# Filling products of TensorE: 256 columns instead of 512, a lower limit on the planned gap, and the whole run

## Chip, cores and metric

One core of a Trainium2 chip runs the program. The time is the device time of one execution in microseconds (us); "the time" of a kernel is the median of its runs. The engines are named as in the profile: PE is TensorE (matrix products), PEld its weight loads, DVE is VectorE, ACT is ScalarE, POOL is GpSimd, SP is the queue that starts the transfers (DMA). PEclk is the share of the full TensorE clock that was granted: 1.00 is 2.4 GHz, 0.50 is 1.2 GHz.

## What is computed

A recurrent attention (RWKV) over 768 steps for 4 batches of 8 heads with 48 channels, and on its output a mixture of four attention experts, two of which are taken per token.

```python
def _attn_ref(r, k, v, w, u):
    for t in range(S):                                  # S = 768
        cur = np.einsum('bhd,bhe->bhde', u[None] * kt, vt)
        y[:, :, t] = np.einsum('bhd,bhde->bhe', rt, state + cur)
        state = wt[:, :, :, None] * state + np.einsum('bhd,bhe->bhde', kt, vt)

def _moe_ref(x, w_gate, wq, wk, wv, wo):                # x: 4 x 768 x 384
    logits = x @ w_gate                                 # 4 experts, the best 2 kept
    for e in range(E):
        q, k, v = x @ wq[e], x @ wk[e], x @ wv[e]       # 64 wide
        a = softmax(causal(scale * (q @ k.T)))
        out += gate[..., e] * (a @ v @ wo[e])
```

## The kernel before

The 768 steps of a batch are cut into two units of 384. For each of the eight units the kernel first does the recurrence in chunks of 64 steps, head pair by head pair (four pairs, a function `one` for each and `far` for two of them), and then the expert stage (`moe`) of the same tokens; the recurrence of unit k+1 is interleaved with the expert stage of unit k.

A head pair of the recurrence goes: load of `lt` (decay, keys, queries; three buffers) and `nat`; two scans on DVE, `suf` (L415) and `pre` (L419); the products `kt` (L422) and `mr` (L424, written into `pre`) on DVE or POOL; on PE the transposes `ktp` (L471), the small products `aps` (L483), `ups` (L502), `yb` (L545), `yi` (L558), and in the first unit `rp` (L439), which reads `lt`; on DVE the state steps `ss` (L510), `am` (L489) and `xi` (L568); then a split into a high and a low part and a transfer `xx<-xs` (L591). The expert stage goes: projections `pp` (L643) and `vp` (L666), scores `sp` (L734), maximum and exponential (L740, L746), transposes `tp` (L759), `yp` (L790), gate (`gp`, `gb`, L824, L835) and output `op` (L862).

The order of all this is worked out on the host by `Plan.order`: each operation has a cost on each engine that may do it, and the planner lays the operations out in time, engine by engine. Every engine then runs its instructions in that order, and semaphores hold an instruction until its inputs and its buffer are there. The planner notes two things of each operation: `o["gap"]`, a pair of the time at which its engine becomes free and the time at which the operation is planned to begin, and `o["new"]`, the buffers that the operation is the first to use, each with the time at which it comes free. PSUM has eight banks, all under one tag (`mo`). On PE an operation whose kind of product differs from the one before is planned 100 ns later (`DRAIN`).

When the instructions are emitted (L928 to L942), a PE operation that opens a PSUM bank can be preceded by filling products: products of a constant (`wz`, zeros and ones in bf16) into the bank that the operation is about to overwrite. They compute nothing that is used. Their number follows from the planned gap t, counted from the later of "PE free" and "bank free". In the kernel before, this is done only where the gap is over 1000 ns and PE becomes free before 60 us of planned time; each product has 512 columns, is counted as 216 ns, and 600 ns at the end of the gap are left empty. At the beginning, 14 products of the same kind (`warm`, L908) run before any real work.

Of the kernel before, what the change touches and what calls it, by code (L numbers as in the profile page):

```python
# [11 lines left out]
F32 = mybir.dt.float32  # L12
# [212 lines left out]
def rwkv_moe(ctx: ExitStack, tc: tile.TileContext, wkr, nat, uN, uT,  # L225
             wqk, wvg, wo, out):
    nc = tc.nc
# [55 lines left out]
    for i in range(NYS):  # L283
        t = cst.tile([128, NH * D + C - D], F32, name=f"ys{i}")
# [620 lines left out]
    wz = one_suf.bitcast(BF16)[:, 0:512]  # L905
# [22 lines left out]
    for o in plan.order(dict(PE=7200.0 - 216 * WARM[0], DVE=1500.0, ACT=2100.0, POOL=3300.0, SP=740.0), SLACK):  # L928
        if o["e"] == "PE" and any(s.bank for _, s in o["new"]):
            at, s = next(x for x in o["new"] if x[1].bank)  # L930
            a, t = o["gap"]
            t -= max(a, at)
            if s.dt == F32 and t > 1000 and a < 60000:
                for _ in range(int((t - 600) / 216)):
                    nc.tensor.matmul(s()[:, 0:512], wz[:, 0:128], wz, start=True, stop=True)
        r = o["fn"](o["e"])
        if r is not None and o["kind"] in BOTH.get(o["e"], ()):
            if o["e"] == "DVE":
                held = r.ins
            elif held is not None:  # L940
                tc.add_manual_dep(r.ins, held.name, mybir.DependencyInfo(mybir.DependencyClass.Sync, mybir.DependencyReason.SCHED_ONLY),
                                  reason="one reader of SBUF's second port at a time")  # L942
# [109 lines left out]
```

## Time and profile before

| | |
|---|---|
| three runs | 346.18, 349.37, 351.52 us; median 349.37 us |
| the profiled execution, its own time | 345.97 us |
| its span, first to last instruction | 344.2 us |
| mean granted TensorE clock | 0.985 |
| busy: PE, DVE, ACT, POOL | 94%, 89%, 69%, 42% of the span |
| filling products (L935) | 49, all between 18.5 and 43 us |

The span lies inside the profiled execution's own time; 1.8 us lie around it. Busy times come from the profiled execution alone. The end of a product in the trace is modelled and lies behind the moment at which the next product can start, so the idle times given in brackets are shorter than the time in which PE has nothing to issue.

### The profile page before, as it was taken

What the parts mean: (1) busy time and instruction counts of PE and PEld (TensorE: products, weight loads), DVE (VectorE), ACT (ScalarE), POOL (GpSimd) and SP (SyncE); (2) the same over time, 40 slices, a digit from 0 to 9 for tenths busy, and PEclk for the clock granted to TensorE, in tenths of its full rate; (3) what the DMA queues carried; (4) which work ended last, traced back from release to release, by engine and by line L of the source; (5) the groups of instructions that cost most, each with busy time, mean ns of one, the idle gap of its engine ahead of it and who ended that gap; (6) DMA issues with size and microseconds to landing.
All of it is one profiled execution on the core that took longest, in us unless ns stands there. A gap on an engine that the chain in (4) does not pass through costs nothing.

```text
span 344.2 us, 13063 instructions
## 1 busy us (share of the span) xinstructions
PE 322.4 (94%) x5118; PEld 266.2 (77%) x5118; DVE 305.5 (89%) x1003; ACT 237.7 (69%) x726; POOL 145.7 (42%) x275
## 2 busy tenths in 40 slices
PE   7698969899999899999999999999999889999996
PEld 2555559679877788897787888898797769898884
DVE  7979979998999989999989999999999998646861
ACT  1686675976778867874966675974885567735872
POOL 3025353652852447423844444646854344121110
PEclk9769999999999999999999999999999999999999
DMA  7562855522624526161726342562543300300101
GB/s 280 176 216 60 269 150 172 164 48 71 211 104 151 182 83 214 36 196 26 233 75 196 104 141 81 154 194 79 166 146 72 116 4 4 105 0 4 70 0 70
DMA packets 15759, 41.50 MB, mean 121 GB/s; under 512 B 2385, under 2 KB 7634, under 8 KB 15698
## 3 DMA queue, kind: packets, MB, share of 16 engines
q1 hardware_dynamic: 15698, 40.67, 37.8%
q8 instruction: 40, 0.66, 0.8%
q14 instruction: 21, 0.17, 0.1%
HBM read 33.58 MB, written 4.72 MB: 111 GB/s over the span
## 4 chain that ended last, share of the span: by engine, by line
PE 68%; DVE 18%; DMA 4%; ACT 3%; issue 3%; SPq 1%; POOL 1%; DVEq 0%; POOLq 0%; ACTq 0%
PE pp L643 13%; PE yp L790 10%; PE tp L759 10%; PE vp L666 8%; PE op L862 8%; PE sp L734 7%; DMA lt<-in_wkr_dram 3%; DVE a L740 3%; PE aps L483 3%; DVE ss L510 2%; PE yi L558 2%; PE yb L545 2%; PE ups L502 2%; DVE suf L415 2%; DVE pre L419 2%
## 5 line engine op out<-in xcount | busy, mean ns | idle before, releaser
L746 ACT ACTIVATE a<-a,mx 128x128 f32<-128x128 f32 (+5 forms) x96 | 63.9, 668 | 12.8 <-DVE mx L740 12.4
L643 PE MATMUL pp<-xx,wh_qk 128*128 128x384 f32 (+2 forms) x216 | 57.7, 333 | 1.4 <-DMA xx<-xs 1.1
L759 PE MATMUL tp<-ident,a 128*128 128x128 f32 x336 | 48.3, 278 | 3.5 <-ACT a L746 1.1
L459 ACT ACTIVATE am<-ident,rk 128x64 f32<-128x64 f32 x174 | 44.7, 339 | 9.2 <-DVE rk L452 8.8
L759 PEld LDWEIGHTS tp<-ident,a 128*128 128x128 f32 x336 | 37.6, 141 | 10.0 <-ACT a L746 2.3
L740 DVE CUSTOM_DVE_ANT_0 a<-sp,cmask 128x384 f32<-128x384 f32 (+4 forms) x96 | 43.6, 497 | 0.4 <-PE sp L734 0.2
L643 PEld LDWEIGHTS pp<-xx,wh_qk 128*128 128x128 f32 x216 | 38.5, 188 | 2.3 <-DMA xx<-xs 1.3
L243 ACT COPY ATa<-tp 128x512 f32<-128x512 f32 (+3 forms) x73 | 32.5, 474 | 6.8 <-PE tp L759 6.8
L510 DVE SCALAR_TENSOR_TENSOR ss<-ss,suf,ups 112x48 f32<-112x48 f32 x160 | 35.9, 258 | 1.3 <-PE ups L502 0.3
L790 PE MATMUL yp<-ATa,v_sb 128*64 128x384 f32 (+2 forms) x256 | 35.0, 413 | 0.1
L643 PE MATMUL pp<-xx,wl_qk 128*128 128x384 f32 (+2 forms) x108 | 35.0, 324 | 0.0
L448 POOL TENSOR_TENSOR nat<-nat,u_sb 128x288 f32<-128x288 f32 x26 | 20.8, 804 | 33.2 <-PE yi L558 8.0
L422 POOL TENSOR_TENSOR kt<-lt,suf 128x384 f32<-128x384 f32 x24 | 23.8, 997 | 24.6 <-PE yb L545 14.4
L415 DVE TENSOR_TENSOR_SCAN suf<-lt,one_suf 128x390 f32<-128x390 f32 x32 | 31.1, 977 | 2.8 <-DMA lt<-in_wkr_dram 2.6
L419 DVE TENSOR_TENSOR_SCAN pre<-lt,inv_pre 128x390 f32<-128x390 f32 x32 | 31.0, 969 | 0.1
L666 PE MATMUL vp<-wh_vg,xx 128*128 128x260 f32 x144 | 29.6, 291 | 0.0
L790 PEld LDWEIGHTS yp<-ATa,v_sb 128*64 128x64 f32 x256 | 16.4, 136 | 14.4 <-issue 11.1
L734 PE MATMUL sp<-Kh,Qh 64*128 64x384 f32 (+4 forms) x128 | 26.5, 361 | 0.9 <-DVE ss L510 0.7
L666 PEld LDWEIGHTS vp<-wh_vg,xx 128*128 128x128 f32 x144 | 23.5, 189 | 0.1
L734 PE MATMUL sp<-Kl,Qh 64*128 64x384 f32 (+4 forms) x128 | 23.6, 325 | 0.0
L734 PE MATMUL sp<-Kh,Ql 64*128 64x384 f32 (+4 forms) x128 | 22.8, 319 | 0.0
L579 POOL TENSOR_TENSOR xx<-xi,xx 112x384 fp32r<-112x384 f32 x16 | 16.1, 1013 | 11.8 <-ACT xx L577 6.4
(354 smaller groups left out, 816.7 us busy)
## 6 DMA issues: line engine op xcount, KB each, us to landing
lt<-in_wkr_dram SPq DMA_DIRECT2D x31, 579.5 KB, 4.9
nat<-in_nat_dram SPq DMA_DIRECT2D x28, 432.0 KB, 3.7
out_dram<-ob SPq DMA_DIRECT2D x24, 192.0 KB, 1.9
xx<-xs SPq DMA_DIRECT2D x48, 48.0 KB, 2.2
w_qk<-in_wqk_dram SPq DMA_DIRECT2D x1, 768.0 KB, 6.5
nat<-in_nat_dram SPq DMA_DIRECT2D x4, 152.0 KB, 5.5
w_vg<-in_wvg_dram SPq DMA_DIRECT2D x1, 390.0 KB, 5.5
lt<-in_wkr_dram SPq DMA_DIRECT2D x1, 384.0 KB
```

Source lines behind the costliest of these rows:

```text
L243: nc.scalar.copy(o, i)
L415: plan.add("suf", {"DVE": t_scan(wb)}, lambda e: nc.vector.tensor_tensor_scan(rev(suf(), wb), rev(w_(), wb), rev(one_suf, wb), 0.0, op0=AL ...
L419: plan.add("pre", {"DVE": t_scan(wb)}, lambda e: nc.vector.tensor_tensor_scan(pre()[:, 0:wb - 1], w_()[:, 0:wb - 1], flat(inv_pre[:, 0:nh] ...
L459: nc.scalar.mul(am()[:, h, i], ident2, rk()[:, i, h:h + 1])
L510: nc.vector.scalar_tensor_tensor(sv(c + 1), zero[0:112] if c == s0 == 0 else sv(c), sfv()[0:112, c, 0:1], ups[c % 2]()[0:112, c // 2 * D:( ...
L643: nc.tensor.matmul(pp()[:, 0:W], w[:, qk, k, cs], xx()[:, x, k, x0:x0 + W], start=(k == j == 0), stop=(k == j == 2))
L666: nc.tensor.matmul(vp()[:, 0:260], xx()[:, x, k, o], w[:, k, :], start=(k == j == 0), stop=(k == j == 2))
L734: nc.tensor.matmul(sps[x]()[:, 0:w], q()[p, t], k()[p, o], start=j == 0, stop=j == 2)
L740: plan.add("max", {"DVE": t_dve(w) + T_RED}, lambda e, x=x, a=a, mx=mx, h=h, o=o, m=m, sps=sps: nc.vector.tensor_tensor_reduce(a()[:, o], ...
L746: plan.add("exp", {"ACT": t_exp(n)}, lambda e, x=x, y=y, mx=mx, a=a: nc.scalar.activation(a()[:, 0:n], a()[:, 0:n], AF.Exp, bias=mx[-1](), ...
L759: nc.tensor.transpose(tp()[:, j * 128:(j + 1) * 128], a()[:, (j0 + j) * 128:(j0 + j + 1) * 128], ident)
L790: nc.tensor.matmul(yp()[e * 64:e * 64 + 64, lo:W], v_sb[ep]()[:, j, e * 64:e * 64 + 64], at, start=(j == 0), stop=(j == nj - 1))
```

## The change

The filling products become half as wide (256 columns), the planned gap needs to be over 450 ns instead of 1000 ns, the limit at 60 us of planned time goes away, and the number of products is the gap less 250 ns, divided by 110 ns, instead of the gap less 600 ns, divided by 216 ns. The plan itself, the order of all other instructions and the engines they run on stay.

```diff
             a, t = o["gap"]
             t -= max(a, at)
-            if s.dt == F32 and t > 1000 and a < 60000:
-                for _ in range(int((t - 600) / 216)):
-                    nc.tensor.matmul(s()[:, 0:512], wz[:, 0:128], wz, start=True, stop=True)
+            if s.dt == F32 and t > 450:
+                for _ in range(int((t - 250) / 110)):
+                    nc.tensor.matmul(s()[:, 0:256], wz[:, 0:128], wz[:, 0:256], start=True, stop=True)
```

## Rows read from the trace of the kernel before

**Rows 1.** The page: busy time, share of the span and number of instructions of the engines; the granted clock in 40 equal slices; and the shares of the engines in the chain that ended last.

```profile
PE 322.4 (94%) x5118; PEld 266.2 (77%) x5118; DVE 305.5 (89%) x1003; ACT 237.7 (69%) x726; POOL 145.7 (42%) x275
...
PEclk9769999999999999999999999999999999999999
...
PE 68%; DVE 18%; DMA 4%; ACT 3%; issue 3%; SPq 1%; POOL 1%; DVEq 0%; POOLq 0%; ACTq 0%
```

**Rows 2.** Windows of 1 us, PE alone: length, PE busy (instructions begun), granted clock, share of the DMA engines, GB/s.

```profile
9.00:10.00 1.00, 0.00 (x0) 1.00 0.74 307
...
12.00:13.00 1.00, 0.71 (x42) 0.93 0.00 0
13.00:14.00 1.00, 1.00 (x43) 0.50 0.95 158
...
22.00:23.00 1.00, 1.00 (x14) 0.50 0.44 154
23.00:24.00 1.00, 1.00 (x78) 0.95 0.07 26
...
27.00:28.00 1.00, 0.09 (x5) 1.00 0.57 215
...
44.00:45.00 1.00, 0.00 (x0) 1.00 0.50 163
```

**Rows 3.** The instructions of the filling line, L935: count, then shortest, median and longest duration in ns, first and last start in us, shapes.

```profile
L935 PEld LDWEIGHTS <-one_suf x49: 95/98/152, 18.5 to 42.9; 128*128 128x128 bf16 x49
L935 PE MATMUL aps<-one_suf x26: 379/379/389, 28.8 to 37.1; 128*128 128x512 bf16 x26
L935 PE MATMUL ktp<-one_suf x14: 376/379/379, 40.3 to 43.1; 128*128 128x512 bf16 x14
L935 PE MATMUL yb<-one_suf x9: 634/634/634, 18.7 to 22.1; 128*128 128x512 bf16 x9
```

**Rows 4.** Timeline of PE, 8 to 45 us: start, length, instruction, count. The four groups of filling products, and two operations behind the first.

```profile
18.71 4.05 PE L935 MATMUL yb<-one_suf 128*128 128x512 bf16 x9
22.69 1.09 PE L545 MATMUL yb<-pre,ys 48*64 48x64 f32 x48
...
25.63 0.55 PE L471 MATMUL ktp<-ident,kt 128*128 128x128 f32 x3
...
28.79 4.06 PE L935 MATMUL aps<-one_suf 128*128 128x512 bf16 x18
...
35.57 1.90 PE L935 MATMUL aps<-one_suf 128*128 128x512 bf16 x8
...
40.34 3.18 PE L935 MATMUL ktp<-one_suf 128*128 128x512 bf16 x14 [0.34 <-DVE xi L568]
```

**Rows 5.** Timeline of all engines, 30 to 52 us: the operations that the second, third and fourth group stand before, and what these wait for.

```profile
32.20 0.52 DVE L424 TENSOR_TENSOR pre<-lt,pre 128x384 f32<-128x384 f32 x1
...
32.77 0.44 PEld L483 LDWEIGHTS aps<-pre,kt 64*64 64x64 f32 x24 [0.42 <-DVE pre L424]
...
37.02 0.54 DVE L422 TENSOR_TENSOR kt<-lt,suf 128x384 f32<-128x384 f32 x1
...
37.62 0.44 PEld L483 LDWEIGHTS aps<-pre,kt 64*64 64x64 f32 x24 [0.64 <-DVE kt L422]
...
45.09 0.31 PEld L471 LDWEIGHTS ktp<-ident,kt 128*128 128x128 f32 x3 [2.06 <-POOL kt L422]
```

**Rows 6.** Waits of PE from 60 us on: engine, tile and line that waited, what for, us in total, times, longest.

```profile
PE yi L558 <- DVE am L489: 1.2, 1, 1.2
PE tp L759 <- ACT a L746: 1.1, 3, 0.7
PE tp L759 <- DVE ss L510: 1.0, 1, 1.0
PE yb L545 <- issue: 0.8, 1, 0.8
PE tp L759 <- ACT am L459: 0.7, 1, 0.7
PE sp L734 <- DVE ss L510: 0.7, 2, 0.4
PE yi L558 <- issue: 0.6, 1, 0.6
PE op L862 <- DVE ss L510: 0.4, 1, 0.4
...
PE pp L643 <- DVE xi L568: 0.2, 1, 0.2
```

**Rows 7.** Timeline, 3 to 30 us: PE operations of the first unit that had waited (idle time in brackets).

```profile
7.85 0.52 PE L471 MATMUL ktp<-ident,kt 128*128 128x128 f32 x3 [1.00 <-DVE kt L422]
...
10.16 0.55 PE L471 MATMUL ktp<-ident,kt 128*128 128x128 f32 x3 [1.29 <-DVE kt L422]
...
16.00 1.06 PE L483 MATMUL aps<-pre,kt 64*64 64x64 f32 x22 [0.81 <-DVE am L489]
```

**Rows 8.** The chain that ended last, in order of time: start, us, what. A part of the first 60 us.

```profile
16.00 0.97 PE aps L483 x20
...
17.16 0.56 PE rp L439 x17
...
17.75 5.57 DMA lt<-in_wkr_dram
...
26.51 0.43 DVE kts L245
...
28.85 3.99 PE aps L935 x18
...
34.91 6.22 DMA lt<-in_wkr_dram
...
52.49 3.27 PE vp L666 x27
```

**Rows 9.** Groups of instructions by line: the weight loads of `vp` (busy us, mean ns of one, idle before).

```profile
L666 PEld LDWEIGHTS vp<-wh_vg,xx 128*128 128x128 f32 x144 | 23.5, 189 | 0.1
```

## Prediction

> **What bounds the kernel now.** I read the page first: its busy shares, its clock and the chain that ended last [rows 1]. PE is busy for 94% of the span and holds 68% of the chain. From 50 us to the end it has hardly a free moment, so what is put on PE there either fits into a real gap or moves the end. In the first 50 us it is otherwise: the chain goes through loads of `lt`, DVE's scans and, in one place, the filling products themselves [rows 8].
>
> The clock row says how much a filling product can still bring. It has a digit under 9 only in slices 2 and 3. In windows of 1 us [rows 2] it falls in the window from 12 to 13 us (0.93), stands at 0.50 (1.2 GHz) from 13 us to 23 us and is back in the window from 23 to 24 us (0.95). Before it fell, PE had worked in short bursts with waits of 1.00 and 1.29 us between them [rows 7], one whole window without an instruction; before it rose, PE ran the first group of nine filling products back to back [rows 4]. After that every digit is 9, and stretches that are almost empty, as from 27 to 28 us and from 44 to 45 us, did not bring it down (1.00 [rows 2]). So behind 24 us there is no clock to win back in this execution; the products put there can only be free or cost.
>
> **The change, part by part.**
>
> *How many products.* The old counts [rows 3, 4] give the planned gaps: n products mean a gap t from 600 + 216n to 600 + 216(n+1) ns. With 9, 18, 8 and 14 that is 2544 to 2760, 4488 to 4704, 2328 to 2544 and 3624 to 3840 ns. By the new rule, (t - 250)/110, they become 20 to 22, 38 to 40, 18 to 20 and 30 to 32: about 110 half-wide products for 49 wide ones.
>
> New gaps in the first 60 us: those of the first unit [rows 7] got no product before, so they were planned under 1000 ns, and each can get 1 to 6. I take four gaps with three each, 12 (none, if all are planned under 450 ns; 36, if there are six with six).
>
> New gaps behind 60 us: the profile shows real waits, not planned ones, so I take the real ones as a measure [rows 6]. They are 14 waits, 7.1 us in all. A wait in brackets is short by what a product's modelled end reaches past the next start: 379 ns [rows 3] less the 222 ns below, 0.16 us. Of those listed, the two marked "issue" lie within an operation, where no planned gap can be. The six longest of the rest (1.2, 1.0, 0.7, 0.7, 0.4, 0.4) would give 10 + 8 + 5 + 5 + 2 + 2 = 32 products. With a few that the plan has and the run has not I take 40 in ten places. Bounds: none, or 85 (7.1 us and 14 times 0.16 us, 9.3 us, all filled). In all about 160, bounds about 106 and 230.
>
> *What one costs.* At full clock 18 wide ones took 3.99 us [rows 8], 222 ns each; half of that, 111 ns, is the lower bound. The nearest row of that width is `vp` with 260 columns: 27 in 3.27 us [rows 8], 121 ns, the upper bound. I take 116 ns, between the two, which is more than the 110 ns that the rule counts. At half clock nine took 3.98 us [rows 4], 442 ns each, so 221 ns for half the width.
>
> The weight load of a filling product is 98 ns, 152 ns at half clock [rows 3], almost as long as the half-wide product. I cost it at nothing: at `vp`, loads of 189 ns [rows 9] hide behind products that follow each other at 121 ns. The Trainium skill, "TensorE: Matmul & The Clock Gate", section "What overlaps and what doesn't", says that a weight load overlaps running products only when it goes to another group of rows; it speaks against half-wide products, since there are twice as many loads. The rows here disagree: both the 222 ns and the 121 ns are for products that use all rows. By the page a product would cost 98 + 116 = 214 ns; by the rows it is 116 ns, and the sum goes by these.
>
> *The four old groups.* The second is on the chain [rows 8]. The `aps` behind it began at 32.77; its input `pre` was ready at 32.72, and the 18 products ended at about 28.79 + 3.99 = 32.78 [rows 4, 5]. They fit exactly. Now 39 of 116 ns take 4.52 us and end at 33.31: 0.54 us later (38 of 111 ns: 0.24; 40 of 121 ns: 0.85). What is late next is `yb`, `yi` and `rp` behind `aps`, then the load of `lt` at 34.91, which waits for its buffer, and the chain to 41 us. I take +0.54. The third: 19 take 2.20 us and end at 37.77, against a start of `aps` at 37.62, whose `kt` came at 37.56 [rows 5]; 0.15 us late (0 to 0.4), but the chain is then in the `lt` load, from 34.91 to 41.13 [rows 8], so nothing; without that cover, the 0.15. The fourth: 31 take 3.60 us and end at 43.94, while `ktp` waits for POOL's `kt` until 45.09 [rows 5]; nothing. The first runs at half clock: 21 of 221 ns take 4.64 us instead of 3.98, 0.66 us more. Behind it `ktp` ended at 26.18 [rows 4], and DVE's copy `kts` is on the chain at 26.51 [rows 8]; 0.33 us are slack, +0.3 is left (0 to 0.6).
>
> *The small early gaps.* Three products are 0.35 us at full clock and 0.66 us at half; the wait before `aps` at 16.00, on the chain, is 0.81 us [rows 7, 8]. Three fit. Six at half clock are 1.33 us, 0.5 us too long. I take +0.1.
>
> *Behind 60 us.* Planned gaps are not real ones, and three old groups at full clock show how far off they are. The second was planned 0.56 to 0.77 us longer than it was (28.79 to 32.72, 3.93 us), the third 0.34 to 0.55 us longer (35.57 to 37.56, 1.99 us), the fourth about 1 us shorter [rows 4, 5]. The 600 ns left empty before covered these errors just about; 250 ns do not. Two in three overran, with 250 ns left by about 0.3 us. So ten places x 2/3 x 0.3 us = 2.0 us, of which PE's share of the chain, 68%, makes +1.4 us. Lower bound 0 (all in real gaps); upper bound 40 x 116 ns = 4.6 us with none in a gap, 9.9 us with 85.
>
> *Sum:* 0.54 + 0.3 + 0.1 + 1.4 = +2.3 us. On the profiled execution's 345.97 us that is 348.3 us. This execution lies below all three timed runs, so I add the same step to their median: 349.37 + 2.3 = 351.7 us.
>
> **The rivals.**
>
> *The clock stays up in the beginning.* The new products between 9 and 18 us could fill just the waits after which the clock fell [rows 2, 7]. Then `aps` and `rp` before the `lt` load at 17.75 (16.00 to 17.73 on the chain [rows 8]) take half of their 1.73 us, the load starts 0.87 us earlier, and the first group ends sooner than before. With +0.54 of the second group: 349.0 us; with all the late cost too, 350.5 us. For it: it rose after a group of such products. Against it: a dozen short ones are 1.4 us at full clock in some 6 us with long waits for DVE. The Trainium skill, same page, section "What's actually happening", says that the slow clock is the default and activity releases it; the trace agrees in that the clock rose after the nine products [rows 2, 4], but whether a dozen hold it no run here shows.
>
> *Everything hidden.* If the plan's late gaps are real and DVE is what ends last around 33 us too, only the order of a few tenths is left: 349.4 us.
>
> *Slower by over 2%: many more planned gaps than real ones, where PE is the chain.* It decides from 7.0 us on the path, 60 of the 116 ns products. For it: the lower limit and the whole run leave nothing of the plan's errors uncovered, and 85 products would be 9.9 us, 359.3 us. Against it: the order was planned with the same errors, and where PE waits elsewhere it catches up.
>
> *The loads do not hide.* 160 products at 98 ns more are 15.7 us of PE; with half of it on the path the time is about 359.5 us. This is the page's rule on weight loads as a mechanism of this kernel; the 121 ns of `vp` speak against it.
>
> **How the numbers follow.** My forecast, a few us slower through overruns: 0.57, with a range of its own from 349.6 (0.24 us and nothing else) to 356.1 us (0.85 + 0.6 + 0.5 + 4.6 = 6.6 us). Clock held: 0.18. Hidden: 0.11. Many overruns: 0.12. Loads exposed: 0.02. Three runs of one kernel spread over 5.3 us, so about 2% is what a measurement here can tell from no change. The range goes from 347.0 us (clock held, with a little of that spread) to 356.5 us; beyond it lie the two slow cases and a rest below. Faster by over 2% (under 342.4 us) has no mechanism here, 0.02 for what I do not see; slower by over 2% (over 356.4 us) 0.14, the two slow cases; within 2% 0.84. Forecast: no change that can be told, 351.7 us.
>
> **What would show it.** Right: about 160 products on the filling line at 111 to 121 ns each; `aps` after the second group at 33.0 to 33.6 us, no longer waiting for `pre`; some 40 products behind 60 us, several followed at once by their operation with no wait. Wrong: a granted clock at 1.00 between 13 and 18 us (clock rival); products more than 200 ns apart at full clock (loads); under 20 products behind 60 us (hidden) or over 80 (slow).

## The result, and the profile after

The changed kernel took 350.70 us (median of 22 runs, 346.28 to 353.15), the kernel before 349.12 us on the same chip (22 runs, 344.32 to 353.48). The ratio is 1.0073, with a 95% interval from 1.0045 to 1.0101: about 2.5 us slower by that ratio (1.6 to 3.5), inside the 2% that were called no change. The ratio leaves out runs that took over 1.5% longer than the fastest of their kernel; over all runs the medians are 1.6 us apart (1.0045).

The profiled execution after took 351.46 us with a span of 349.6 us. It must not be held against that of before without care: 351.46 us is 0.8 us above its kernel's median, 345.97 us was 3.2 us below its own. The pair of profiles therefore shows 5.4 us between the spans where the medians show 1.6 us. What the profiles show is places; how much is read from the timed runs.

The page of the profile after, beside [rows 1]: busy time and number of instructions, granted clock in 40 slices, shares of the chain that ended last.

```profile
PE 329.8 (94%) x5230; PEld 276.5 (79%) x5230; DVE 306.7 (88%) x1003; ACT 237.2 (68%) x726; POOL 145.3 (42%) x275
...
PEclk9968999999999999999999999999999999999999
...
PE 64%; DVE 19%; DMA 7%; ACT 3%; issue 2%; POOL 2%; SPq 1%; DVEq 0%; POOLq 0%; ACTq 0%
```

PE has 112 instructions more, 161 filling products for 49, and 7.4 us more of busy time. DMA's share of the chain went from 4% to 7%; loads of `nat` and `xx` have 3% each now, where the load of `lt` had 3% before.

The instructions of the filling line after, beside [rows 3]: count, shortest, median and longest duration in ns, first and last start in us.

```profile
L935 PEld LDWEIGHTS <-one_suf x161: 95/98/152, 8.8 to 344.8; 128*128 128x128 bf16 x161
L935 PE MATMUL aps<-one_suf x59: 272/273/421, 30.7 to 67.9; 128*128 128x256 bf16 x59
L935 PE MATMUL ktp<-one_suf x35: 269/273/283, 8.8 to 47.3; 128*128 128x256 bf16 x35
L935 PE MATMUL yb<-one_suf x22: 421/421/421, 18.7 to 23.2; 128*128 128x256 bf16 x22
...
L935 PE MATMUL op<-one_suf x8: 272/272/283, 344.1 to 344.9; 128*128 128x256 bf16 x8
```

The four old groups have 22, 39, 18 and 30 products; 31 stand in eight new gaps planned before 60 us, and 21 in six behind it (five before `tp`, two `sp`, one `ups`, two `tp`, three `sp`, eight `op`).

Timeline of PE after, beside [rows 4]: the same four groups, and two new small ones.

```profile
18.71 4.90 PE L935 MATMUL yb<-one_suf 128*128 128x256 bf16 x22
23.54 1.16 PE L545 MATMUL yb<-pre,ys 48*64 48x64 f32 x48
...
26.68 0.71 PE L935 MATMUL ups<-one_suf 128*128 128x256 bf16 x5
...
28.17 0.61 PE L935 MATMUL ups<-one_suf 128*128 128x256 bf16 x4
30.20 0.56 PE L502 MATMUL ups<-nat,kts 64*64 64x48 f32 x24 [1.43 <-DMA nat<-in_nat_dram]
30.70 6.10 PE L935 MATMUL aps<-one_suf 128*128 128x256 bf16 x39
36.72 0.58 PE L483 MATMUL aps<-pre,kt 64*64 64x64 f32 x24
...
39.52 2.14 PE L935 MATMUL aps<-one_suf 128*128 128x256 bf16 x18
41.59 0.58 PE L483 MATMUL aps<-pre,kt 64*64 64x64 f32 x24
...
44.18 3.44 PE L935 MATMUL ktp<-one_suf 128*128 128x256 bf16 x30
```

The first group ends 0.85 us later than before (`yb` at 23.54 for 22.69). The third `ups`, at 30.20, now waits 1.43 us for a load of `nat`; in the kernel before it began at 28.29, and the profile names DVE as what it waited for. But the same load had landed just ahead of it there too. The load's issue (number, length in ns, start in us) and its time to landing, in the kernel before:

```profile
L251 SPq DMA_DIRECT2D nat<-in_nat_dram x1: 536/536/536, 24.7 to 24.7; - x1
...
DMA to landing us min/median/max: 3.5/3.5/3.5
```

It landed at 28.16 us, 0.13 us before this `ups`. In eleven of the twelve traces that record this landing the third `ups` begins 0.13 or 0.14 us behind it, in the kernel before and after among them: this load sets when it begins. Of the 1.91 us by which `ups` is later after the change, 0.91 us come from a later start of the load and 1.00 us from its longer time to landing, 4.50 us for 3.50.

The second group then takes 6.10 us, and `aps` behind it begins 3.95 us later than in [rows 5].

The chain after, in order of time (start, us, what), beside [rows 8].

```profile
18.92 4.69 PE yb L935 x22
23.61 1.09 PE yb L545 x47
24.70 0.70 PE yi L558 x46
25.40 0.17 PE ktp L471
25.57 4.50 DMA nat<-in_nat_dram
...
30.20 0.56 PE ups L502 x19
30.76 6.03 PE aps L935 x39
36.79 0.51 PE aps L483 x24
...
38.86 5.98 DMA lt<-in_wkr_dram
...
56.94 3.26 PE vp L666 x27
```

Read downward: the first group holds `yb` and `yi`, the load of `nat` cannot start before `yi` has read the buffer (in the kernel before, too, SP's queue stood 5.5 us before that load for `yi`), `ups` waits for the load, and the second group follows. At `vp` the pair is 4.45 us apart (56.94 for 52.49).

Windows of 1 us after, PE alone, beside [rows 2]: length, PE busy (instructions begun), granted clock, DMA share, GB/s.

```profile
16.00:17.00 1.00, 1.00 (x41) 1.00 0.72 274
17.00:18.00 1.00, 0.31 (x20) 0.63 0.99 366
...
24.00:25.00 1.00, 1.00 (x77) 0.95 0.02 8
...
29.00:30.00 1.00, 0.00 (x0) 1.00 0.03 14
30.00:31.00 1.00, 0.80 (x27) 0.96 0.00 0
31.00:32.00 1.00, 1.00 (x7) 0.50 0.00 0
...
34.00:35.00 1.00, 1.00 (x10) 0.83 0.00 0
```

Two things differ from the profile before. The clock fell in the window from 17 to 18 us, not from 12 to 13. And it fell a second time, to 1.2 GHz, inside the second group, after a microsecond in which PE began nothing: 39 products took 6.03 us instead of the 4.5 us of the forecast.

### The profile page after: what moved, and what is told of

The parts are those of the page before. It is cut to its first block, busy times and chain, and to the rows that moved or that the text cites. A ratio compares the mean times of both kernels' runs of the same rounds, so it can differ in the third digit from the quotient of the medians.

```text
span 349.6 us, 13280 instructions
## 1 busy us (share of the span) xinstructions
PE 329.8 (94%) x5230; PEld 276.5 (79%) x5230; DVE 306.7 (88%) x1003; ACT 237.2 (68%) x726; POOL 145.3 (42%) x275
## 4 chain that ended last, share of the span: by engine, by line
PE 64%; DVE 19%; DMA 7%; ACT 3%; issue 2%; POOL 2%; SPq 1%; DVEq 0%; POOLq 0%; ACTq 0%
PE pp L643 14%; PE tp L759 9%; PE yp L790 8%; PE op L862 7%; PE vp L666 7%; PE sp L734 6%; DVE a L740 3%; DMA nat<-in_nat_dram 3%; DMA xx<-xs 3%; DVE ss L510 3%; DVE pre L419 2%; PE yi L558 2%; PE yb L545 2%; PE ups L502 2%; DVE suf L415 2%
## 5 line engine op out<-in xcount | busy, mean ns | idle before, releaser
L734 PE MATMUL sp<-Kh,Qh 64*128 64x384 f32 (+4 forms) x128 | 25.2, 362 | 0.2 <-DVE ss L510 0.2
L734 PE MATMUL sp<-Kl,Qh 64*128 64x384 f32 (+4 forms) x128 | 22.5, 322 | 0.0
L734 PE MATMUL sp<-Kh,Ql 64*128 64x384 f32 (+4 forms) x128 | 22.1, 319 | 0.0
L568 DVE TENSOR_TENSOR xi<-yi,xi 112x192 f32<-112x192 f32 x64 | 18.9, 346 | 3.0 <-ACT xi L243 2.7
```

The source lines that it names most:

```text
L734: nc.tensor.matmul(sps[x]()[:, 0:w], q()[p, t], k()[p, o], start=j == 0, stop=j == 2)
```

## The experiments

**Theory A:** the loss arises before 60 us. The products of the large groups are too many for their real gaps, the first group above all, behind which `yb`, `yi` and the load of `nat` are late. **Theory B:** it arises behind 60 us, from planned gaps that the run does not have. **Theory C:** the small early products stand on the path. **Theory D,** formed after the first four runs: more instructions in PE's queue move the places at which the profile shows PE waiting for nothing but "issue". Two further readings, **E** (the first group is hidden) and **F** (the 13 late products by themselves), stand as rivals where they are named. Ratios are to the kernel before on the same chip, with 95% intervals; 0.1% is 0.35 us. Edits marked "after" are to the changed kernel, the others to the kernel before. In the latter the old rule stays for all gaps not named.

**The parts of the change.** Only what is planned before 60 us, 140 products (after):

```
-            if s.dt == F32 and t > 450:
+            if s.dt == F32 and t > 450 and a < 60000:
```

> The new rule kept, but only where TensorE becomes free before 60 us of planned time: 135 filling products, none later. Theory A (the loss arises in the first 60 us: the products of the two large groups are too many, and the first group delays yb, yi and a load of nat): close to the changed kernel, 0.4 to 0.8 us under it, so about 350.0 us or ratio 1.005 to the kernel before. Theory B (most of the loss is the late overruns, +1.4 us of the forecast): 1.4 us or more under the changed kernel, about 349.2 us, no difference from the kernel before.

Measured: 348.58 against 347.43 us, 1.0025 (0.9990 to 1.0061), some 0.9 us. Timeline of PE of this kernel:

```profile
18.70 4.44 PE L935 MATMUL yb<-one_suf 128*128 128x256 bf16 x22
...
28.98 0.56 PE L502 MATMUL ups<-nat,kts 64*64 64x48 f32 x24 [0.22 <-DVE ss L510]
29.47 4.43 PE L935 MATMUL aps<-one_suf 128*128 128x256 bf16 x39
33.83 0.58 PE L483 MATMUL aps<-pre,kt 64*64 64x64 f32 x24
```

Here the clock did not fall in the second group: the same 39 products take 4.43 us. The third `ups` is 0.69 us later than before and `aps` 1.06 us, which agrees with the time. Of the 0.69 us, 0.20 us are a later start of the load of `nat` and some 0.5 us its longer time to landing (3.98 us).

Only what is planned behind 60 us, 21 products, beside the old rule before it:

```
+            if s.dt == F32 and a >= 60000 and t > 450:
+                for _ in range(int((t - 250) / 110)):
+                    nc.tensor.matmul(s()[:, 0:256], wz[:, 0:128], wz[:, 0:256], start=True, stop=True)
```

> The old rule in the first 60 us of planned time (49 products of 512 columns), the new rule only behind it: 26 products of 256 columns, 8 of them in front of the last output product. Theory A: 0.5 us over the kernel before, all of it at the end, ratio 1.0015. Theory B: 1.4 us over it, ratio 1.004.

Measured: 1.0130 (1.0083 to 1.0176), 351.47 us, from six runs. That speaks for B and is more than the whole change costs. The trace has 21 products where the expectation counted 26.

Only the new short gaps before 60 us (450 to 1000 ns, 31 products), with the old groups as before:

```
+            if s.dt == F32 and a < 60000 and 450 < t <= 1000:
+                for _ in range(int((t - 250) / 110)):
+                    nc.tensor.matmul(s()[:, 0:256], wz[:, 0:128], wz[:, 0:256], start=True, stop=True)
```

> The four old groups with 49 products of 512 columns as before; new products of 256 columns only in planned gaps of 450 to 1000 ns of the first 60 us. Theory A: these alone do not harm, and hold the clock up to about 17 us instead of 13 us, so the load of lt before 18 us starts about 0.4 us earlier: between 0.5 us under the kernel before and equal to it. Theory C (the small products are what is on the path, in front of the first unit's state steps): 1 to 2 us over the kernel before.

Measured: 1.0001 (0.9962 to 1.0039). The 1 to 2 us of C are not seen; up to 1.4 us lie inside the interval. The mean granted clock of the timed runs rose from 0.977 to 0.982, and no time came of it that can be told. Timeline of PE of this kernel:

```profile
29.49 0.56 PE L502 MATMUL ups<-nat,kts 64*64 64x48 f32 x24 [1.50 <-DMA nat<-in_nat_dram]
```

So the third `ups` can be as late as this, 1.20 us behind the kernel before, with the first group as it was: the load started 0.39 us later, since the clock rose only at 24 us, and took 4.30 us to land.

Only the longer old groups (after: 22, 39, 18 and 30 products, nothing else):

```
-            if s.dt == F32 and t > 450:
+            if s.dt == F32 and a < 60000 and t > 1000:
```

> Only the four old groups, with the new count and width: 22, 39, 18 and 30 products of 256 columns, gaps over 1000 ns of the first 60 us. Theory A: carries most of the loss, 1.5 to 2.5 us over the kernel before, ratio 1.004 to 1.007; the first group at half clock takes 4.9 us and yb starts 0.9 us later. Theories B and C: within 0.5 us of the kernel before.

Measured: 1.0133 (1.0079 to 1.0186), 351.73 us, from six runs, mean clock 0.972. With the small products beside them (the first run above) the same groups cost 0.25%, without them 1.3%. The parts do not add up. Timeline of PE of this kernel:

```profile
31.86 7.03 PE L935 MATMUL aps<-one_suf 128*128 128x256 bf16 x39
```

The second group ran at 1.2 GHz here (clock 0.50 from 31 to 37 us) and took 7.03 us, 4.43 us in the first run. And over all timed runs the kernels fall into two sets: the mean granted clock was 0.972 to 0.978 in those without the small early products, the kernel before among them, and 0.982 to 0.986 in those with them. In the profiles the clock was at 1.2 GHz within the second group in six of the eight kernels without, in one of the six with them. So the small products can hold back what the long groups cost without them. This fits, but the profiled execution is the slowest of its six runs (355.38 us), and no run shows the size.

**Which of the large groups.** The first group cut from nine products to four:

```
-                for _ in range(int((t - 600) / 216)):
+                n = 4 if o["kind"] == "yb" else int((t - 600) / 216)
+                for _ in range(n):
```

> The kernel before with only the first group cut from 9 to 4 products of 512 columns; all else as before. Theory A (in the kernel before, the first group at half clock takes 4.0 us where 2 were planned, and yb, yi, a load of nat and the ups at 28.3 us hang on its end): yb starts at about 21 us instead of 22.7, and the kernel gains 1 to 1.7 us, ratio 0.995 to 0.997. Theory E (the length of the first group is hidden behind DVE): no difference, ratio 1.000; or a loss, if the clock then comes back later.

Measured: 346.51 against 348.12 us, 0.9957 (0.9915 to 0.9999). Timeline of PE of this kernel (one record of the group is missing):

```profile
20.02 0.63 PE L936 MATMUL yb<-one_suf 128*128 128x512 bf16 x1
20.87 1.06 PE L936 MATMUL yb<-one_suf 128*128 128x512 bf16 x2 [0.22 <-issue]
21.86 1.56 PE L545 MATMUL yb<-pre,ys 48*64 48x64 f32 x48
...
28.13 0.56 PE L502 MATMUL ups<-nat,kts 64*64 64x48 f32 x24 [0.73 <-DMA nat<-in_nat_dram]
...
33.50 0.58 PE L483 MATMUL aps<-pre,kt 64*64 64x64 f32 x24 [0.82 <-DVE pre L424]
```

From the group's first product to the third `ups` it is 8.11 us here, 9.58 us before, 10.28 us in the first run above and 11.49 us after. So even the nine products of the kernel before were too many, by an interval that just leaves 1 out. Of the 1.47 us between this and the kernel before only 0.58 us are left at `aps` (13.48 for 14.06 us), which then waits 0.82 us for DVE's `pre`.

The second group alone, 39 half-wide products for 18 (`aps`, `t > 4000`):

> The kernel before with only the second group changed from 18 products of 512 columns to 39 of 256. By the forecast's term aps starts 0.54 us later where the clock is full and about 0.6 us more where it is half: 0.5 to 1.2 us over the kernel before, ratio 1.0015 to 1.0035. If the second group is what costs 1.3% in the run with all four new groups, ratio over 1.008.

Measured: 1.0044 (0.9994 to 1.0093). It leans to a loss and does not settle its size.

**Behind 60 us.** The late products without the last eight before `op` (`o["kind"] != "op"` added to the second edit):

> The kernel before, and behind 60 us the 13 new products of 256 columns without the 8 in front of the last output product. Theory A and the sizes of the gaps: 0 to 0.5 us over the kernel before, ratio 1.000 to 1.0015. Theory D (it is not the products' time but that more instructions in TensorE's queue move the places where it runs empty, the waits marked issue): about as slow as the run with all late products, ratio 1.008 or more.

Measured: 1.0069 (1.0030 to 1.0107), 2.4 us, for 13 products that are 1.45 us of PE. That is above what A allows (1.0015); the 1.008 of D lies inside the interval. Its trace has an "issue" wait at 242.22 us; that of the second run has one at 241.68 us, in the same place of the program.

No late products, and the fourth group as 28 half-wide for 14 wide, which adds only 14 products in a gap with room:

```
+            if s.dt == F32 and t > 1000 and a < 60000 and o["kind"] == "ktp":
+                for _ in range(2 * int((t - 600) / 216)):
+                    nc.tensor.matmul(s()[:, 0:256], wz[:, 0:128], wz[:, 0:256], start=True, stop=True)
```

> The kernel before with the fourth group as 28 products of 256 columns instead of 14 of 512: the same 3.1 us in a gap that ends with a wait of 1.6 us anyway, and 28 more instructions in TensorE's queue for all that follows. Theories A and B: no difference, ratio 1.000. Theory D: the waits marked issue come at other places, and the time moves by 1 us or more either way.

Measured: 1.0029 (0.9984 to 1.0074). Inconclusive between D and nothing.

The 13 late products, and 32 half-wide ones in the fourth group, so that the queue is another:

> The 13 products behind 60 us of the earlier run without the last group, and in the fourth group 32 products of 256 columns for 14 of 512 (3.5 us in a gap of 4.7 us), so that 31 products more than in the kernel before stand in TensorE's queue before 240 us instead of 13. Theory D (the place where the queue runs empty follows from the number of instructions, and at 13 to 21 more it falls into a yi near 241 us): no issue wait in that yi, the stretch from the gate's transpose near 240 us to the next one takes 45 us instead of 47 to 50, ratio 1.000 to 1.002 in spite of more products. Theory F (the 13 products themselves are what costs): ratio 1.006 to 1.008 as in the earlier run.

Measured: 1.0062 (1.0028 to 1.0097). The loss of the 13 products stays. But the "issue" wait in `yi`, which was to go, stays too, so the run does not part the products' own time from D. The timeline rows with "issue", first of the second run (late products alone), then of this one, then of the run before it, which has no late products:

```profile
241.68 0.21 PE L558 MATMUL yi<-am,nat 64*64 64x64 f32 x1 [1.13 <-issue]
```

```profile
245.10 0.56 PE L558 MATMUL yi<-am,nat 64*48 64x64 f32 x19 [0.73 <-issue]
```

```profile
245.06 0.34 PE L558 MATMUL yi<-am,nat 64*64 64x64 f32 x5 [1.22 <-issue]
```

Counted through the traces, the wait stands at the 3858th to 3863rd product of PE in all six kernels that have one between 237 and 246 us, with 70 to 91 of them filling or starting products (a few records are missing). So D is right about the place: it goes with the number of products issued, and the operation that waits moves with it, by up to 18 products. What the wait costs is another matter: kernels with such a wait and no late products were at 1.0029 (the run before this one), 1.0044 (the second group alone) and, below, 0.9966. So a price of the wait is not seen; that D has a part in the loss is not excluded.

**Versions that should be better.** First group four wide ones, the 31 small products, the fourth group nine wide and ten half-wide, the rest as before, nothing late:

```
+            elif s.dt == F32 and t > 1000 and a < 60000 and o["kind"] == "yb":
+                for _ in range(4):
+                    nc.tensor.matmul(s()[:, 0:512], wz[:, 0:128], wz, start=True, stop=True)
+            elif s.dt == F32 and t > 1000 and a < 60000 and o["kind"] == "ktp":
+                for _ in range(9):
+                    nc.tensor.matmul(s()[:, 0:512], wz[:, 0:128], wz, start=True, stop=True)
+                for _ in range(10):
+                    nc.tensor.matmul(s()[:, 0:256], wz[:, 0:128], wz[:, 0:256], start=True, stop=True)
```

> A version put together from the parts that help: the first group cut to 4 products of 512 columns, new products of 256 columns only in gaps of 450 to 1000 ns of the first 60 us (31), the fourth group as 9 of 512 and 10 of 256; 31 products more than in the kernel before. Theories A and D together: as the run with the short first group or better, since the clock is up for longer and no issue wait falls into the yi near 241 us: ratio 0.992 to 0.996. If the small products give nothing: 0.996. If the short first group lets the clock stay at half for the second group: 1.000 or more.

Measured: 347.07 against 348.35 us, 0.9954 (0.9917 to 0.9991). It is 0.5% under the kernel before, and no faster than the short first group alone (0.9957). Its trace does not show the gain where A puts it: `ups` comes 10.62 us after the group's first product, since the nine small products between the `ups` took 1.27 and 0.84 us there, at 1.2 GHz (clock 0.50 from 26 to 29 us), 0.71 and 0.61 us in the changed kernel. That it is the first group here too rests on the timed runs.

The same columns with the small ones joined to wide ones, so that the queue has 62 filling products:

> The same columns in the same gaps, but the new small products put together in twos, 512 columns wide: the same filling time with 13 instead of 31 products more than in the kernel before. Theory D: issue waits of about 1 us in yb near 117 us and yi near 241 us as in the runs with 13 more, and 1 to 3 us over the version with 31 more. Theories A and F, for which only the filled time counts: equal to it.

Measured: 0.9966 (0.9917 to 1.0014), not to be told from the version before it. Its trace has an "issue" wait of 0.64 us in `yi` at 237.92 us, that of the version before it none behind 60 us.

The changed kernel with eight products for 22 in the first group, and the fourth as 44 of 128 columns, so that the queue stays at 161 (after):

```
+            if s.dt == F32 and t > 1000 and a < 60000 and o["kind"] == "yb":
+                for _ in range(8):
+                    nc.tensor.matmul(s()[:, 0:256], wz[:, 0:128], wz[:, 0:256], start=True, stop=True)
+            elif s.dt == F32 and t > 1000 and a < 60000 and o["kind"] == "ktp":
+                for _ in range(44):
+                    nc.tensor.matmul(s()[:, 0:128], wz[:, 0:128], wz[:, 0:128], start=True, stop=True)
```

> The changed kernel with only the first group cut from 22 to 8 products of 256 columns, and the fourth group as 44 of 128 columns instead of 30 of 256, so that the number of products in the queue stays 161. Theory A: the first group ends up to 3.1 us earlier (14 products of 221 ns), the load of nat and ups behind it too: 1.5 to 3 us under the changed kernel, ratio to the kernel before 0.998 to 1.003. Theory E (the first group is hidden): ratio 1.007 as the changed kernel.

Measured: 347.79 against 348.35 us, 0.9998 (0.9961 to 1.0034), where the changed kernel had 1.0073 (1.0045 to 1.0101). Fourteen products fewer before `yb` take back 0.75% (0.3 to 1.2), some 2.6 us, with all late products still there. The fourth group was changed with them, in a gap with room. E falls: the first group is not hidden. In the trace the third `ups` begins 8.38 us behind the group's first product, 11.49 us in the changed kernel. But eight half-wide products are less than the nine wide ones of the kernel before. So the run shows that the group's length sets the time, and not that the 0.85 us by which the change lengthened it made the loss; that was not timed alone. All that the change did before 60 us is bounded by the first run, 0.25% (−0.10 to 0.61).

## Why the prediction was right

It said 351.7 us and no change that can be told, by a step of +2.3 us; measured were 350.70 us and about +2.5 us (1.6 to 3.5). That overruns cost a few us was right; that the sum came so close is in part luck, as the terms show. (The upper end of the forecast's own range, 349.37 + 6.6, is 356.0, not 356.1.) Step by step:

**Counts and price: right.** The old groups got 22, 39, 18 and 30, all within the ranges given. Before 60 us there were 31 new ones, not 12, behind it 21, not 40; the total of 161 for "about 160" is two errors that cancel. 39 products in 4.37 us in the chain of the first run are 112 ns each, 116 ns was taken; at the lower clock 221 ns was taken, and the 22 from 18.71 to 23.54 us are 220 ns each. The weight loads, of 98 ns, were hidden behind products that follow each other at 112 ns. The Trainium skill, "TensorE: Matmul & The Clock Gate", section "What overlaps and what doesn't", says that a weight load overlaps running products only when it goes to another group of rows; the estimate by that rule was 214 ns a product, and the measurement decides against it for products that use all rows.

**The first group, +0.3: the length right, the place and the size wrong.** The prediction followed it to DVE's copy `kts` and found 0.33 us of slack there. The path goes through `yb` and `yi` to the load of `nat`, and has no such slack: the third `ups` begins 0.13 us behind that load's landing in the kernel before, and 2.6 us (difference of the two ratios) went when the group was cut to eight. The row that was missed is SP's wait of 5.5 us for `yi` before that load. Missed with it is that the load's time to landing is not constant: it was 3.4 to 5.0 us in the traces, also with the first group as before, and half or more of the delay at `ups` came from it. What lengthens it stays open, and so does what the longer group costs by itself.

**The second group, +0.54: right at full clock.** In the first run the group itself is 0.37 us longer than before (4.43 for 4.06). Timed alone it is +1.5 us, between −0.2 and +3.2; its trace has the group at 1.2 GHz for a part (6.00 us), for which the prediction had no term. Its sign that `aps` would begin at 33.0 to 33.6 us did not come: 33.83 us in the first run, 36.72 us after. **The third and fourth, nothing:** the fourth ended long before `ktp`; the third was not tried alone.

**The small early gaps, +0.1: right.** They cost nothing that can be told (1.0001), although there were 31.

The three early terms together, 0.94 us, are what the first run measured (0.9 us, −0.3 to +2.1).

**Behind 60 us, +1.4: right within what was measured, by fewer products and more overruns.** It expected ten places, two in three of them with an overrun of 0.3 us. The timelines show six, five with an overrun. PE after, at the one free place and at the first on the path, and at the end, first after, then before:

```profile
78.85 0.72 PE L935 MATMUL tp<-one_suf 128*128 128x256 bf16 x5
...
104.88 0.39 PE L935 MATMUL sp<-one_suf 128*128 128x256 bf16 x2 [0.29 <-DVE ss L510]
105.20 0.51 PE L734 MATMUL sp<-Kh,Qh 64*128 64x512 f32 x2
...
343.59 0.61 PE L790 MATMUL yp<-ATb,v_sb 128*64 128x128 f32 x8
344.13 1.05 PE L935 MATMUL op<-one_suf 128*128 128x256 bf16 x8
344.93 0.42 PE L862 MATMUL op<-wh_o,yh 128*128 128x384 f32 x1
```

```profile
338.65 0.61 PE L790 MATMUL yp<-ATb,v_sb 128*64 128x128 f32 x8
339.19 0.44 PE L862 MATMUL op<-wh_o,yh 128*128 128x384 f32 x1
```

The five before `tp` lie in a real wait. The two before `sp` themselves wait for the release of the bank they write, and `sp` begins 0.32 us behind them: the product needs the same bank, so it can't fill that wait, it only follows it. How much later each operation begins, counted from the start of the operation ahead of it and against the same operation in the kernel before: 0.21 us (`sp`), 0.74 (`ups`, of it 0.46 a wait of the product for its bank), 0.16 (`tp`), 0.43 (`sp`), and 0.47 us from the end of `yp` to the end of the span (5.01 us before, 5.48 us after; the plan there waits for both halves of `yh`, the run for one). The sum is 2.0 us, the larger part of what the change costs; with the 13 products alone it is 1.0 us. In the pair of profiles the kernels drift apart by some 0.9 us between `vp` at 57 us and the end (4.45 to 5.4 us), and "issue" waits of 1.4 us before and 1.0 us after lie in that stretch. The timed runs give 1.7 us (0.1 to 3.2) between the first run and the whole change, and 2.4 us (1.0 to 3.7) for 13 products. The first agrees with the sum of 2.0 us, the second reaches down to its 1.0 us; whether more than the overruns is lost is not shown. Why the 21 alone came out at 1.3% stays open; their profiled execution also has a fall of the clock behind 60 us (0.50 in the window from 278 to 280 us).

**The rivals.** That the clock stays up came half true, and with it most of one of the prediction's own signs of being wrong, a clock of 1.00 between 13 and 18 us: it fell 4.4 us later, but at the same 18.71 us began the first group, at 1.2 GHz as before, and no time was won. DVE's `am` and `ss`, not PE, were the chain ahead of it. What no rival had is the second fall of the clock in the second group: 6.03 us instead of 4.4 us, 1.6 us of the 4.45 us in the pair of profiles. It can't be booked to the change: kernels whose products before 60 us are those of the kernel before showed it too (the runs with late products alone and with 13 of them, 5.30 and 5.52 us for the second group's 18 products, 4.06 us before), and the first run did not. Nor was the kernel before free of it, as far as the clock tells: its profiled execution has a mean clock of 0.985, its timed runs beside the experiments 0.975 to 0.977. That no clock can be won back behind 24 us held for that one execution; it need not hold for the kernel. Many overruns and exposed loads did not come: there were 21 products behind 60 us, and 112 ns each.

## What to carry to other kernels

A filling product is free only if the operation that it stands before is still waiting for something else when the product ends, and a gap in a plan is no proof of that: follow what stands behind that operation in other queues, since here, with a load of `nat` behind the next two operations, taking away 14 products gained 2.6 us. Where the wait is for the release of the bank that the filling product writes, it can't fill the wait at all. When a kernel's own executions spread by 2 to 3%, read places from the profiles and sizes from timed runs, part by part, and expect that the parts need not add up. Hold the clock of the one profiled execution against that of the timed runs before you take it for the kernel's.

## What the runs showed of the hardware

The granted clock fell within a run of back-to-back products, at 31 us after a microsecond without a PE instruction, in some executions and not in others. It also fell between 60 and 340 us in seven of the fourteen traces (0.50 in the window from 278 to 280 us of the run with late products alone). In the 92 timed runs of the kernel before beside the experiments, three series, 0.01 less of mean clock goes with some 4 us more (correlation −0.75 to −0.85 in each series). That does not show which of the two causes the other. A higher mean clock (0.982 for 0.977) with the small products alone gave no shorter time that can be told (1.0001, 0.9962 to 1.0039).

The time from the issue of one and the same load of `nat` to its landing was 3.4 to 5.0 us in twelve traces; in eleven of them the product that waited for it began 0.13 or 0.14 us behind.

Inside dense runs of small products PE sometimes waits 0.3 to 1.2 us for "issue" alone. The place goes with the number of products that PE has issued, and not with the operation: the 3858th to 3863rd in six kernels (237.92 to 245.10 us), the 2989th in both kernels with 161 filling products (185.79 and 183.51 us). Not every kernel waits there, and three show no such wait behind 60 us. What the engine waits for stays open.
